# Packed attention and a softplus FFN on one core: batch 0's FFN in two halves around batch 1's

## The chip, the core and the metric

One core of one Trainium2 chip runs the kernel. The metric is device time in microseconds (us), the median of several runs; in the profile, times are counted from the first instruction of the span. Engines: PE (TensorE), DVE (VectorE), ACT (ScalarE), POOL (GpSimd) and SP (SyncE, which here issues nearly all DMAs).

## The reference

```python
def _attn_ref(q, k, v, p):                      # q, k, v: 8 batches, 8 heads, 576 rows, 64 columns
    def sm_attn(qq, kk, vv):                    # softmax attention, scale 1/8
...
    p_packed = sm_attn(p, k, v)                 # p: 32 rows a head
    return sm_attn(q, p_packed, p_packed)

def _moe_ref(x, w_in, w_out):                   # x: 4608 x 512, w_in: 512 x 2048, w_out: 2048 x 512
    h = x @ w_in
    g = np.maximum(h, 0.0) + np.log1p(np.exp(-np.abs(h)))
    return (g @ w_out).astype(np.float32)
```

For each batch, 32 pack rows attend to k and v; then q attends to the 32 packed rows. The heads side by side are x, which goes through a feed-forward net (FFN) with softplus. q, k, v and p come as 32-bit floats, w_in and w_out as 64-bit floats.

## The kernel before, in words

**FFN units.** A batch has 576 rows, and the hidden size 2048 is cut into 16 tiles of 128 (`NF`). A unit (b, f) is one tile of one batch. `gemm1` (L609) makes 12 matmuls 128x288 into two PSUM halves `ph`: softmax weights `at_h`, `at_l` against `mh`, `ml`, the packed rows already multiplied by w_in (`make_m`, L572 to L588). Products are kept exact enough by splitting each factor into a high and a low part, three products each. `softplus` takes abs, exp and ln on ACT (L631, L633, L634), the sum on DVE (L636), copies the last 64 rows to `rest` on POOL (L640) and splits the other 512 into `gh` and `gl` on DVE (L623, L624). Two units later (`LAG`), `gemm2_tile` (L647) adds `gh`, `gl` times `wo_h`, `wo_l` to four accumulators `acc`, three matmuls 128x512 each. There are two `ph` banks, so unit f+1's first half waits for DVE's L636 of unit f. After a batch's last tile, `store` (L662) copies each `acc` to SBUF (L664) and SP writes it out. Each pair of batches has one more accumulator for the `rest` rows.

**Attention ahead.** While a batch's FFN runs, the next batch's attention is done in small steps (`attention_next`, 29 steps), drawn `PACE` = 0.56 steps per accumulator tile. Batch 0's (`attention_first`) comes before all FFN work. `weights` (L545) splits the second softmax's result `aT` into `at_h` (ACT, L554) and `at_l` (DVE, L555), which `gemm1` of that batch needs.

**Conversion.** w_in and w_out are read as 64-bit floats and turned into 32-bit ones in 32 items of 128x512 (`convert`): 16 column blocks of w_in (`i0` to `i15`) and 16 row blocks of w_out (`o0` to `o15`), in the order i0, i1, o0, o1, i2, i3, and so on, counted from 0. An item is a DMA into a buffer `x`, two ACT steps (`m` L204, `r` L208), two DVE steps (`t` L210, L215), one POOL sum (L223), and for w_out a cast on ACT (`wo_h`, L242) and a difference on DVE (`wo_l`, L248). From item 8 on, two buffers of tag `x` hold the items in flight; stores use the same two. Unit (b, f) needs items i`f` and o`f`. Batch 0's FFN draws the conversion's steps at `CONV` = 1.6 per accumulator tile, so all 32 items lie in attention 0 and in batch 0's units.

**What sets the order.** PE and SP keep the program's order. DVE, ACT and POOL get theirs from a scheduler that simulates a timeline when the program is built; from then on it is fixed, and each engine takes its instructions strictly in that order.

## Time and profile before

| | us |
|---|---|
| median of 3 runs (lowest, highest) | 802.3 (802.19, 803.24) |
| profiled execution | 800.31 |
| its span | 798.5 |
| PE busy in the span | 734.1 |
| DVE busy | 542.9 |
| ACT busy | 430.8 |

The time of an execution is the span and 1.8 us around it. A busy PE is not a PE at its peak: the granted clock tells how fast its matmuls run. Unit starts are read from PE's chain: twelve L609 matmuls begin a unit. Batch 0's unit 0 begins at 51.76 us, unit 4 at 95.51, unit 8 at 122.81; batch 1's unit 0 at 173.85, batch 2's at 257.96, batch 3's at 351.87, batch 4's at 434.56.

### The profile page before, as it was taken

Reading aid. Unit: us, or ns where it says so; the run is one execution under the profiler, and the core shown is the slowest. Engines: PE = TensorE matmul, PEld = TensorE weight load, DVE = VectorE, ACT = ScalarE, POOL = GpSimd, SP = SyncE. Lnnn points to the kernel's source line nnn. Section 1 sums busy time; section 2 is a strip of 40 time slices with the busy share of each in tenths; the row PEclk is TensorE's granted clock in tenths of the full one; section 3 lists DMA queues with packets and bytes.
Section 4 is the critical chain, followed back from the end, with each engine's and each line's share of the span. In section 5 each row is a group of like instructions: output and inputs, shape, how many; then the busy total and the mean of one; then the engine's idle time right before and its main releaser. Section 6 shows DMA issues by size and latency. Waiting matters only on the chain.

```text
span 798.5 us, 14178 instructions
## 1 busy us (share of the span) xinstructions
PE 734.1 (92%) x5312; PEld 576.1 (72%) x5312; DVE 542.9 (68%) x1228; ACT 430.8 (54%) x1073; POOL 93.5 (12%) x166
## 2 busy tenths in 40 slices
PE   6423798999999999999999999999999999999997
PEld 3302666676878877887778877887788778778886
DVE  2697787786587666867586666866686656775554
ACT  5646768455546264565555264566456265555540
POOL 1334424100000000010001000010000000000010
PEclk9655799999999999999999999999999999999999
DMA  9979746107310362007200452008200500010002
GB/s 222 237 154 222 188 97 177 37 1 142 61 31 1 83 103 67 1 1 152 58 23 2 106 80 68 1 27 146 61 1 1 126 1 2 1 53 1 1 1 66
DMA packets 168244, 55.96 MB, mean 70 GB/s; under 512 B 134896, under 2 KB 161520, under 8 KB 168176
## 3 DMA queue, kind: packets, MB, share of 16 engines
q1 hardware_dynamic: 167904, 55.00, 31.3%
q8 instruction: 41, 0.67, 0.3%
q14 instruction: 27, 0.22, 0.1%
q10 hardware_dynamic: 272, 0.07, 0.0%
HBM read 45.61 MB, written 9.44 MB: 69 GB/s over the span
## 4 chain that ended last, share of the span: by engine, by line
PE 71%; DVE 10%; DMA 9%; ACT 6%; issue 2%; SPq 1%; POOL 0%; DVEq 0%; ACTq 0%; POOLq 0%
PE acc L647 36%; PE ph L609 23%; PE acc_m L647 6%; DMA x_i<-in_moe_w_in 4%; PE psm L572 3%; DMA x_o<-in_moe_w_out 2%; PE ps L284 2%; DMA v<-in_v 2%; DVE e L636 1%; ACT e L631 1%; ACT e L633 1%; PE psp L327 1%; PE psa L317 1%; DVE t L210 1%; DVE at_l L555 1%
## 5 line engine op out<-in xcount | busy, mean ns | idle before, releaser
L631 ACT ACTIVATE e<-ph 128x288 f32<-128x288 f32 x256 | 102.4, 403 | 201.4 <-PE ph L609 181.5
L647 PE MATMUL acc<-wo_h,gh 128*128 128x512 f32 x512 | 207.8, 406 | 0.2 <-DVE o L664 0.2
L647 PE MATMUL acc<-wo_l,gh 128*128 128x512 f32 x512 | 201.6, 394 | 0.0
L647 PE MATMUL acc<-wo_h,gl 128*128 128x512 f32 x512 | 200.9, 392 | 0.0
L636 DVE SCALAR_TENSOR_TENSOR e<-ph,e 128x288 f32<-128x288 f32 x256 | 113.3, 450 | 121.2 <-ACT e L634 119.9
L609 PE MATMUL ph<-at_h,mh 128*128 128x288 f32 x512 | 160.7, 314 | 34.0 <-DVE e L636 18.2
L609 PE MATMUL ph<-at_l,mh 128*128 128x288 f32 x512 | 154.4, 302 | 3.6 <-DVE at_l L555 3.6
L609 PE MATMUL ph<-at_h,ml 128*128 128x288 f32 x512 | 154.2, 301 | 0.0
L609 PEld LDWEIGHTS ph<-at_h,mh 128*128 128x128 f32 x512 | 98.7, 193 | 72.3 <-DVE e L636 27.3
L640 POOL COPY rest<-e 128x64 f32<-128x64 f32 x128 | 48.1, 376 | 600.4 <-DVE e L636 534.8
L647 PEld LDWEIGHTS acc<-wo_h,gh 128*128 128x128 f32 x512 | 96.6, 189 | 28.6 <-issue 9.8
L647 PEld LDWEIGHTS acc<-wo_h,gl 128*128 128x128 f32 x512 | 96.5, 188 | 21.1
L633 ACT ACTIVATE e<-e 128x288 f32<-128x288 f32 (+1 forms) x240 | 108.7, 454 | 3.4
L634 ACT ACTIVATE e<-e 128x288 f32<-128x288 f32 (+1 forms) x240 | 108.9, 455 | 2.9
L647 PEld LDWEIGHTS acc<-wo_l,gh 128*128 128x128 f32 x512 | 96.8, 189 | 13.3
L609 PEld LDWEIGHTS ph<-at_l,mh 128*128 128x128 f32 x512 | 98.9, 193 | 7.0 <-DVE at_l L555 4.4
L609 PEld LDWEIGHTS ph<-at_h,ml 128*128 128x128 f32 x512 | 99.0, 193 | 0.0
L624 DVE TENSOR_TENSOR gl<-e,gh 128x512 fp32r<-128x512 f32 x128 | 89.9, 703 | 5.8
L587 ACT CAST mh<-psm 128x512 fp32r<-128x512 f32 (+1 forms) x72 | 35.5, 540 | 51.1 <-PE psm L572 51.0
L588 DVE TENSOR_TENSOR ml<-psm,mh 128x512 fp32r<-128x512 f32 (+1 forms) x72 | 42.6, 625 | 29.7 <-ACT mh L587 29.3
L623 DVE CAST gh<-e 128x512 fp32r<-128x512 f32 x128 | 55.3, 432 | 5.7 <-PE acc L647 0.5
L572 PE MATMUL psm<-w_in_sb,pt 64*32 64x512 f32 (+1 forms) x576 | 38.7, 573 | 2.5 <-DVE a L351 1.7
(72 smaller groups left out, 704.6 us busy)
## 6 DMA issues: line engine op xcount, KB each, us to landing
v<-in_v SPq DMA_DIRECT2D x16, 576.0 KB, 4.9
x_i<-in_moe_w_in SPq DMA_DIRECT2D x32, 256.0 KB, 5.0
x_o<-in_moe_w_out SPq DMA_DIRECT2D x16, 512.0 KB, 4.4
q<-in_q SPq DMA_DIRECT2D x56, 144.0 KB, 3.2
k<-in_k SPq DMA_DIRECT2D x52, 144.0 KB, 3.1
out<-o SPq DMA_DIRECT2D x21, 256.0 KB, 2.1
out<-o SPq DMA_DIRECT2D x10, 192.0 KB, 2.3
w_in_sb<-in_k SPq DMA_DIRECT2D x2, 576.0 KB, 5.9
```

Source lines behind the costliest of these rows:

```text
L572: nc.tensor.matmul(ps[hh * J:(hh + 1) * J, :n], res["pt"][g][o:o + D, hh * J:(hh + 1) * J], w_in_sb[o:o + D, hh, c * n:(c + 1) * n], start ...
L587: nc.scalar.copy(mh[:, cols], ps[:, :n])
L588: nc.vector.tensor_tensor(ml[:, cols], ps[:, :n], mh[:, cols].bitcast(F32), op=ALU.subtract)
L609: nc.tensor.matmul(ph[:, :C], x[:, ms], y[:, g, cs], start=(i == 0), stop=(i == 3 * G - 1),)
L623: nc.vector.tensor_copy(hi, x)
L624: nc.vector.tensor_tensor(lo, x, hi.bitcast(F32), op=ALU.subtract)
L631: nc.scalar.activation(es[c], hv[c], AF.Abs)
L633: nc.scalar.activation(x, x, AF.Exp, scale=-1.0)
L634: nc.scalar.activation(x, x, AF.Ln, bias=1.0)
L636: nc.vector.scalar_tensor_tensor(es[c], hv[c], 0.0, es[c], op0=ALU.max, op1=ALU.add)
L640: nc.gpsimd.tensor_copy(rest[:, rest_at(b, f), r:r + REST], e[:, NT * P:])
L647: nc.tensor.matmul(acc, x[:, cs], y[:, f, :], start=(first and i == 0), stop=(last and i == 2),)
```

## The change

- **Order of FFN units** (`runs`): batch 0's tiles 0 to 7, batch 1's 0 to 15, batch 0's 8 to 15, then batches 2 to 7 as before. After tile 7, batch 0's four accumulators are stored to the output; near the end `fetched` reads them back and the last store adds them (`part`).
- **Attention:** batch 1's runs in batch 0's first eight units (`PACE_FIRST` = 0.95), batch 2's from batch 1's tile 8 on (0.56). k of batch 1 is loaded within attention 0. In attention 0, the transposes of q come together and the second softmax is taken for two chunks next to each other.
- **Conversion:** 1.1 steps per accumulator tile until done, with its instructions at a priority lower by 150 for the scheduler.
- **Buffers:** the turned k and q and the weights `at_h`, `at_l` of a batch share two buffers `T0` or `T1`, by batch; items 2, 3, 6 and 7 use `T1` before batch 1 needs it. Turned k of batch 2 goes through the two `x` buffers. Batch 1 makes its `m` for two tiles at a time, like batch 0, no longer for four.
- **Scheduling block:** the simulated timeline covers the program up to batch 2's first unit. There a branch leads into a second block, which the ordinary scheduler orders.

```diff
-    ctx.enter_context(tc.block(schedule_with_timeline_sim=True))
...
-        t = cv.tile([PW, H, D], F32, tag="m", name=f"p_{bg}", bufs=1)
+        t = work.tile([PW, H, D], F32, tag="a1T", name=f"p_{bg}", bufs=1)
...
-        pool, bufs = (cv, 2) if tag == "x" else (work, 1)
+        pool, bufs = (cv, 2) if tag == "x" else (work, 2)
...
-        slots = ["x", "x", "at_h", "at_l"]
+        slots = ["x", "x", "T1", "T1"]
...
+    def place(b):
+
+        return f"T{b if b < 2 else (b + 1) % 2}"
...
-        return work.tile([P, HG, C], F32, tag="T", name=f"T_{nm}_{b}_{g}", bufs=2)
+        return work.tile([P, HG, C], F32, tag=place(b), name=f"T_{nm}_{b}_{g}", bufs=2)
...
-        src, dst = loaded[nm, b, g], turned(nm, b, g)
+        src = loaded[nm, b, g]
+        dst = None if (nm, b) == ("k", 2) else turned(nm, b, g)
+        heads = []
+            two = (
+                cv.tile([P, 2, C], F32, tag="x", name=f"T_{nm}_{b}_{g}_{o}", bufs=2)
+                if dst is None else dst[:, o:o + 2, :]
+            )
...
-        qt = turned("q", b, 0)
-        qT.append(transposed("q", b, 0, 0, qt))
...
-        for hh in range(2, HG):
-            qT.append(transposed("q", b, 0, hh, qt))
-            yield
-        a2 = scores2(b, 0, 0, qT)
-        a2n = scores2(b, 0, 1, qT)
-        yield
...
+        a2 = {}
+        for g in range(G):
+            qt = turned("q", b, g)
+            qT = []
+            for hh in range(HG):
+                qT.append(transposed("q", b, g, hh, qt))
+                yield
+                if (g, hh) == (0, 0):
+                    res[b]["pt"].append(packed_transposed(b, 1, pp[1]))
+                if g and hh < 2:
+                    (softmax2_exp, softmax2_div)[hh](b, 0, 0, a2[0, 0])
+            load("k", b + 1, g)
+            for c in range(2):
+                a2[g, c] = scores2(b, g, c, qT)
+            yield
+        softmax2_exp(b, 1, 0, a2[1, 0])
+        yield
+        softmax2_div(b, 1, 0, a2[1, 0])
+        softmax2_exp(b, 0, 1, a2[0, 1])
+        yield
+        softmax2_div(b, 0, 1, a2[0, 1])
+        softmax2_exp(b, 1, 1, a2[1, 1])
+        yield
+        softmax2_div(b, 1, 1, a2[1, 1])
...
+        def load_next(nm, g):
+            if b > FIRST:
+                load(nm, b + 1, g)
-        load("k", b + 1, 0)
+        load_next("k", 0)
...
-        for nm, g in (("k", 0), ("k", 1), ("q", 0), ("v", 0), ("v", 1), ("q", 1)):
+        if b > FIRST:
+            for nm in ("k", "v"):
+                for g in range(G):
+                    load(nm, b, g)
+                    for _ in range(4):
+                        yield
+            return
+        for nm, g in (("q", 0), ("v", 0), ("v", 1), ("q", 1)):
             load(nm, b, g)
-            for _ in range(4):
+            for _ in range(3):
...
-        at_h = work.tile([P, G, S], F32R, tag="at_h", name=f"at_h_{b}", bufs=1)
-        at_l = work.tile([P, G, S], F32R, tag="at_l", name=f"at_l_{b}", bufs=1)
+        at_h, at_l = (
+            work.tile([P, G, S], F32R, tag=place(b), name=f"{nm}_{b}", bufs=2)
+            for nm in ("at_h", "at_l")
+        )
...
-        return MC if b else MC // 2
+        return MC if b > 1 else MC // 2
...
-        pool, th, tl = (cv, "t", "r") if b and c % 2 == 0 else (work, "mh", "ml")
+        pool, th, tl = (cv, "t", "r") if b > 1 and c % 2 == 0 else (work, "mh", "ml")
...
-    def store(acc, pieces, nm):
-        o = cv.tile([P, DM], F32, tag="x", name=f"o_{nm}", bufs=2)
-        nc.vector.tensor_copy(o, acc)
...
+    def fetched():
+
+        two = [
+            cv.tile([P, 2, DM], F32, tag="x", name=f"part_{i}", bufs=2) for i in range(NT // 2)
+        ]
+        parts = [two[t // 2][:, t % 2, :] for t in range(NT)]
+        for t, o in enumerate(parts):
+            move(o, [(0, 0, t * P, P)], False)
+        return parts
+
+    def store(acc, pieces, nm, part=None):
+        if part is None:
+            o = cv.tile([P, DM], F32, tag="x", name=f"o_{nm}", bufs=2)
+            nc.vector.tensor_copy(o, acc)
+        else:
+            o = part
+            nc.vector.tensor_tensor(o, acc, o, op=ALU.add)
+        move(o, pieces, True)
...
+    HALF = NF // 2
     PACE = 0.56
-    AFTER = 10
-    CONV = 1.6
+    PACE_FIRST = 0.95
+    BEHIND = 150
+    CONV = 1.1
+
+    front = ExitStack()
+    front.enter_context(tc.block(schedule_with_timeline_sim=True))
+
+    def convert_on():
+        with tc.high_priority(offset=-BEHIND):
+            next(conv, None)
...
-            next(conv)
+            convert_on()
...
-    early = loads(FIRST)
-    units = [(b, f) for b in range(B) for f in range(NF)]
-    ahead, chain, due = iter(()), iter(()), 0.0
+    early = iter(())
+    runs = [(0, 0, HALF), (1, 0, NF), (0, HALF, NF)] + [(b, 0, NF) for b in range(2, B)]
+    units = [(b, f) for b, f0, f1 in runs for f in range(f0, f1)]
+    starts = {(b, f0): f1 for b, f0, f1 in runs}
+    ends = {(b, f1 - 1): f0 for b, f0, f1 in runs}
+    ahead, chain, due, pace = iter(()), iter(()), 0.0, 0.0
...
+            if b == 2 and f == 0:
+                front.close()
+            begins = {(0, 0): 1, (1, HALF): 2}.get((b, f), b + 1 if b > 1 and f == 0 else B)
+            if (b, f) == (0, NF - 2):
+                parts = fetched()
+            if (b, f) in ((0, 0), (1, 2)):
+                early = loads(b + 1)
...
+                due, pace = 0.0, PACE if begins > 1 else PACE_FIRST
             chain = softplus(b, f, gemm1(b, f, res[b]), gs)
+            if (b, f) in ends and u + 1 < len(units) and (b, f) != (1, NF - 1):
                 for _ in ahead:
                     pass
-                if b + 1 < B:
-                    weights(b + 1)
+                weights(units[u + 1][0])
...
+            if (b2, f2) in starts:
+                acc = [
+                    ps_acc.tile([P, DM], F32, tag="acc", name=f"acc_{b2}_{f2}_{t}")
+                    for t in range(NT)
+                ]
+        done = u >= LAG and (b2, f2) in ends
+        last = done and f2 == NF - 1 and (b2 == 0 or b2 > 1 and b2 % 2)
...
+                if done:
+                    part = parts[t] if (b2, f2) == (0, NF - 1) else None
+                    store(acc[t], [(0, b2, t * P, P)], f"{b2}_{f2}_{t}", part)
...
-                if b < FIRST:
-                    next(early, None)
-                due += PACE if b >= FIRST or NT * f + t >= AFTER else 0
+                next(early, None)
+                due += pace
...
-                if b == 0:
-                    cdue += CONV
-                    while cdue >= 1:
-                        next(conv, None)
-                        cdue -= 1
+                cdue += CONV
+                while cdue >= 1:
+                    convert_on()
+                    cdue -= 1
```

**How instructions move: ACT around batch 0's unit 4.** `e_0_4` is the softplus of batch 0's tile 4; `m_n` and `r_n` are the two ACT steps of conversion item n, `x_o10` is item 22's buffer. Before:

```order
L204 ACTIVATE m_22_1102<-x_o10_1001 128x512
L208 ACTIVATE r_23_1133<-x_o11_1049 128x512
L631 ACTIVATE e_0_4_822<-ph_0_4_0_808 128x288
L204 ACTIVATE m_23_1131<-x_o11_1049 128x512
L631 ACTIVATE e_0_4_822<-ph_0_4_1_815 128x288
L633 ACTIVATE e_0_4_822<-e_0_4_822 128x576
L242 CAST wo_h_91<-t_22_1106 128x512
L208 ACTIVATE r_24_1178<-x_i12_1108 128x512
L634 ACTIVATE e_0_4_822<-e_0_4_822 128x576
L204 ACTIVATE m_24_1176<-x_i12_1108 128x512
L587 CAST mh_0_3_0_880<-psm_0_3_0_870 128x256
L242 CAST wo_h_91<-t_23_1135 128x512
```

The same place with the change (`a1T_1` and `a1_1` belong to batch 1's attention):

```order
L645 ACTIVATE e_0_3_800<-e_0_3_800 128x576
L328 COPY a1T_1_1_876<-psa_1_1_0_877 96x384
L642 ACTIVATE e_0_4_896<-ph_0_4_0_882 128x288
L642 ACTIVATE e_0_4_896<-ph_0_4_1_889 128x288
L644 ACTIVATE e_0_4_896<-e_0_4_896 128x576
L328 COPY a1T_1_1_876<-psa_1_1_1_906 96x384
L645 ACTIVATE e_0_4_896<-e_0_4_896 128x576
L598 CAST mh_0_3_0_989<-psm_0_3_0_979 128x256
L598 CAST mh_0_3_0_989<-psm_0_3_1_980 128x256
L642 ACTIVATE e_0_5_1009<-ph_0_5_0_995 128x288
L642 ACTIVATE e_0_5_1009<-ph_0_5_1_1002 128x288
L644 ACTIVATE e_0_5_1009<-e_0_5_1009 128x576
```

In both programs items 0 to 21 have their `m` and `r` on ACT ahead of `e_0_4`. Before, items 22 to 25 follow from the middle of `e_0_3` to `e_0_5`; now none stands from there to batch 1's `e_1_2`.

**SP around item 22 (`x_o10`).** Before:

```order
L162 DMA x_i10_933<-in_moe_w_in 64x4x128 x2
L162 DMA x_i11_955<-in_moe_w_in 64x4x128 x2
L162 DMA x_o10_1001<-in_moe_w_out 128x512
L162 DMA x_o11_1049<-in_moe_w_out 128x512
L162 DMA x_i12_1108<-in_moe_w_in 64x4x128 x2
L162 DMA x_i13_1137<-in_moe_w_in 64x4x128 x2
L149 DMA k_2_0_1170<-in_k 32x36x32 x4
L162 DMA x_o12_1182<-in_moe_w_out 128x512
L149 DMA k_2_1_1273<-in_k 32x36x32 x4
L162 DMA x_o13_1290<-in_moe_w_out 128x512
```

With the change (`o_0_7_t` is batch 0's partial sum, accumulator t after tile 7):

```order
L161 DMA x_i10_1232<-in_moe_w_in 64x4x128 x2
L161 DMA x_i11_1280<-in_moe_w_in 64x4x128 x2
L678 DMA out_0<-o_0_7_0_1343 96x512
L678 DMA out_0<-o_0_7_0_1343 32x512
L161 DMA x_o10_1353<-in_moe_w_out 128x512
L678 DMA out_0<-o_0_7_1_1358 64x512 x2
L678 DMA out_0<-o_0_7_2_1367 32x512
L678 DMA out_0<-o_0_7_2_1367 96x512
L678 DMA out_0<-o_0_7_3_1380 96x512
L678 DMA out_0<-o_0_7_3_1380 32x512
L161 DMA x_o11_1391<-in_moe_w_out 128x512
```

The load of item 22 now stands behind the first store of the partial sums, and item 23's behind all of them. On ACT, item 22's `m` and `r` stand within `e_1_2`, batch 1's tile 2, item 23's within `e_1_3`; each has softplus steps behind it in the queue. The buffers alternate, so `o_0_7_2` takes item 22's.

**DVE where batch 1's FFN begins.** Before, `at_l_1` is finished ahead of the softplus sum of batch 0's last tile:

```order
L371 TENSOR_TENSOR a2_1_1_1_1644<-a2_1_1_1_1644,z2_1_1_1_1748 128x288
L588 TENSOR_TENSOR ml_1_0_1_1721<-psm_1_0_1_1707,mh_1_0_1_1720 128x512
L375 STREAM_TRANSPOSE aT_1_1_0_1693<-a2_1_1_0_1637 128x288
L375 STREAM_TRANSPOSE aT_1_1_1_1753<-a2_1_1_1_1644 128x288
L555 TENSOR_TENSOR at_l_1_1756<-aT_1_0_0_1555,at_h_1_1755 128x288
L555 TENSOR_TENSOR at_l_1_1756<-aT_1_0_1_1622,at_h_1_1755 128x288
L555 TENSOR_TENSOR at_l_1_1756<-aT_1_1_0_1693,at_h_1_1755 128x288
L555 TENSOR_TENSOR at_l_1_1756<-aT_1_1_1_1753,at_h_1_1755 128x288
L116 COPY pT_94<-ppt_1_0_1782 64x256
L636 SCALAR_TENSOR_TENSOR e_0_15_1738<-ph_0_15_0_1724,e_0_15_1738 128x288
```

With the change, the end of batch 1's second softmax stands among the last steps of batch 0's tile 7, directly ahead of batch 1's first softplus sum:

```order
L634 CAST gh_0_7_1239<-e_0_7_1183 128x512
L381 TENSOR_TENSOR a2_1_1_0_1124<-a2_1_1_0_1124,z2_1_1_0_1190 128x288
L379 TENSOR_SCALAR z2_1_1_1_1201<-z2_1_1_1_1201 128x9
L635 TENSOR_TENSOR gl_0_7_1240<-e_0_7_1183,gh_0_7_1239 128x512
L385 STREAM_TRANSPOSE aT_1_1_0_1195<-a2_1_1_0_1124 128x288
L380 RECIPROCAL z2_1_1_1_1201<-z2_1_1_1_1201 128x9
L381 TENSOR_TENSOR a2_1_1_1_1131<-a2_1_1_1_1131,z2_1_1_1_1201 128x288
L566 TENSOR_TENSOR at_l_1_1209<-aT_1_1_0_1195,at_h_1_1208 128x288
L385 STREAM_TRANSPOSE aT_1_1_1_1206<-a2_1_1_1_1131 128x288
L566 TENSOR_TENSOR at_l_1_1209<-aT_1_1_1_1206,at_h_1_1208 128x288
L647 SCALAR_TENSOR_TENSOR e_1_0_1262<-ph_1_0_0_1248,e_1_0_1262 128x288
```

From the first transpose of that last softmax group (`a2_1_1_0`) to the last `at_l_1`, 29 DVE instructions stand in this queue; on PE, one more unit (0, 7), three matmuls L647 and one `make_m` stand between the scores that start them and batch 1's first `gemm1`.

More of the change, by code (lines that the diff above doesn't have):

```diff
@@ L499, in attention_next @@
         yield
-        load("k", b + 1, 1)
+        load_next("k", 1)
         a1T = work.tile([NP, SI, P], F32, tag="a1T", name=f"a1T_{b}_1", bufs=1)
@@ L508, in attention_next @@
         yield
-        load("v", b + 1, 0)
+        load_next("v", 0)
         a2 = scores2(b, 0, 0, qT[0])
@@ L514, in attention_next @@
         yield
-        load("v", b + 1, 1)
+        load_next("v", 1)
         softmax2_exp(b, 0, 0, a2)
@@ L660, in rows, with move @@
         return n, o.rearrange("(t c) e -> c t e", c=2)[c, t:t + n, :]
-    def store(acc, pieces, nm):
-        o = cv.tile([P, DM], F32, tag="x", name=f"o_{nm}", bufs=2)
-        nc.vector.tensor_copy(o, acc)
+    def move(o, pieces, to_dram):
         for row, b, col, n in pieces:
             while n:
-                m, dst = rows(b, col, n)
-                nc.sync.dma_start(dst, o[row:row + m, :])
+                m, at = rows(b, col, n)
+                here = o[row:row + m, :]
+                nc.sync.dma_start(*((at, here) if to_dram else (here, at)))
                 row, col, n = row + m, col + m, n - m
+    def fetched():
[14 more added lines that the diff above has]
+        move(o, pieces, True)
     def rests(b):
@@ L754, in pack_attention_then_softplus_ffn @@
             gh, gl = gs.pop((b2, f2))
-            if f2 == 0:
-                acc = [ps_acc.tile([P, DM], F32, tag="acc", name=f"acc_{b2}_{t}") for t in range(NT)]
-        last = u >= LAG and f2 == NF - 1 and b2 % 2 == 1
+            if (b2, f2) in starts:
[5 more added lines that the diff above has]
+        last = done and f2 == NF - 1 and (b2 == 0 or b2 > 1 and b2 % 2)
         if last:
-            both = rests(b2)
+            both = rests(b2 + 1 - b2 % 2)
             next(both)
@@ L763, in pack_attention_then_softplus_ffn @@
                 gemm2_tile(
-                    acc[t], gh, gl, f2, slice(t * P, (t + 1) * P), f2 == 0, f2 == NF - 1
+                    acc[t], gh, gl, f2, slice(t * P, (t + 1) * P), (b2, f2) in starts, done
                 )
-                if f2 == NF - 1:
-                    store(acc[t], [(0, b2, t * P, P)], f"{b2}_{t}")
+                if done:
+                    part = parts[t] if (b2, f2) == (0, NF - 1) else None
+                    store(acc[t], [(0, b2, t * P, P)], f"{b2}_{f2}_{t}", part)
             if u < len(units):
-                if b < FIRST:
-                    next(early, None)
-                due += PACE if b >= FIRST or NT * f + t >= AFTER else 0
+                next(early, None)
+                due += pace
                 while due >= 1:
```

45 lines of the change are left out of this document (10 added, 35 removed).

## The prediction

> **What bounds the kernel now.** I read the page first: its span, the busy times and the slices of 20 us.
>
> ```profile
> span 798.5 us, 14178 instructions
> PE 734.1 (92%) x5312; PEld 576.1 (72%) x5312; DVE 542.9 (68%) x1228; ACT 430.8 (54%) x1073; POOL 93.5 (12%) x166
> PE   6423798999999999999999999999999999999997
> PEclk9655799999999999999999999999999999999999
> ```
>
> PE is the bound from the seventh slice on. Its 64 us of idle time lie almost wholly in the first six slices, where its clock is low too. So only the front can give time back. The view of busy times in stretches, cut at the starts of units, says how much. Its columns are the stretch, its length, then busy time of PE, weight loads, DVE, ACT and POOL, the granted clock and the share of the DMA engines.
>
> ```profile
> 20.00:51.76 31.76, 12.17 (x128) 7.41 (x129) 25.23 (x52) 19.31 (x41) 11.06 (x8) 0.59 0.86 215
> 51.76:95.51 43.75, 20.49 (x104) 15.36 (x105) 34.58 (x67) 27.37 (x53) 17.95 (x15) 0.62 0.86 196
> 95.51:122.81 27.30, 24.60 (x167) 18.57 (x167) 21.52 (x45) 18.37 (x41) 8.13 (x9) 0.91 0.53 114
> 122.81:173.85 51.04, 47.25 (x400) 35.13 (x401) 41.17 (x102) 31.56 (x66) 10.27 (x13) 0.97 0.28 72
> 173.85:257.96 84.11, 82.27 (x622) 64.82 (x622) 58.51 (x135) 47.26 (x125) 5.68 (x16) 1.00 0.28 56
> 173.85:182.64 8.79, 8.79 (x49) 7.79 (x49) 5.56 (x12) 4.89 (x13) 1.12 (x2) 1.00 0.04 10
> 351.87:434.56 82.69, 82.19 (x624) 64.83 (x622) 58.89 (x136) 47.62 (x126) 6.43 (x16) 1.00 0.28 57
> ```
>
> Rows two to four are batch 0's sixteen units: 122.09 us, where batch 3 (last row) takes 82.69 with PE busy all the time. The excess is 39.4 us. The sixth row holds two bare units, without attention: 4.39 us each. Units 0 to 3 take 43.75 where four bare ones take 17.6, so most of the excess, 26 us, lies there. What the first units wait for, the waits from 51.8 to 174 us and the chain from 60 to 140 us show.
>
> ```profile
> PE ph L609 <- DVE e L636: 16.1, 7, 8.1
> ACT r L208 <- DMA x_i<-in_moe_w_in: 6.5, 5, 2.9
> ```
>
> ```profile
> 70.23 6.63 DMA x_i<-in_moe_w_in
> ...
> 78.74 3.91 DMA x_o<-in_moe_w_out
> ...
> 85.93 4.75 DMA x_i<-in_moe_w_in
> ...
> 95.00 0.47 DVE e L636
> ...
> 95.51 3.25 PE ph L609 x12
> ...
> 108.19 2.28 PE acc L647 x9
> ```
>
> PE waits for the softplus sum on DVE, DVE for ACT, and ACT stands at a conversion item whose DMA has not landed, with softplus steps behind it. The conversion's queue position, not its amount, stalls PE here.
>
> **The change part by part.** I sum from unit to unit, against the profiled execution: it took 800.31 us, 1.8 more than its span and 2.0 less than the median of 802.3. Batch 2 starts at 257.96 us; from there on the work is the same, so the change in time is the change of that start, plus what the second block costs.
>
> *A, up to unit 4 of batch 0 (95.51).* On ACT, items 0 to 21 still stand ahead of unit 4's softplus, so the stall of units 0 to 3 isn't removed, only its cause can shrink. DVE is busy for 34.58 of 43.75 us; 9.2 are idle. The change moves the first part of batch 1's attention in here. Its DVE groups (51.8 to 174 us):
>
> ```profile
> L260 DVE STREAM_TRANSPOSE T_q<-q 128x576 f32<-128x576 f32 x4 | 2.9, 752 | 0.0
> L297 DVE TENSOR_REDUCE m<-a 128x1 f32<-128x576 f32 x2 | 1.5, 726 | 0.0
> ```
>
> With small ones that is 2.9 + 1.5 + 0.5 = 4.9 us more. Against it, batch 1's v and its last q leave this stretch: by SP's order they now go out ahead of item 14, mostly between 20 and 51.76 us, where the DMA engines have 14% free, and the three chained landings of 15.3 us get shorter. Bounds: 4.3 earlier (all idle time filled) to 4.9 later (none). I take 1.5 earlier, for the DMA waits are the larger sum: 94.0.
>
> *B, units 4 to 7.* Before: 27.30 us, with conversion items and a little attention. Now no conversion step stands there, but batch 1's attention must end there. Four bare units are 17.6; attention and its matmuls cost 82.69 − 16 × 4.39 = 12.4 us a batch, half of it here: 6.2. At the end PE waits for `at_l_1`: 29 DVE instructions, at 58.89 / 136 = 0.43 us each 12.6 us, while PE has one bare unit, three matmuls L647 (2.28 / 9 × 3 = 0.8) and one `make_m` of 0.95, 6.1 in all; the latter from
>
> ```profile
> L572 PE MATMUL psm<-w_in_sb,pt 64*32 64x256 f32 (+1 forms) x96 | 5.7, 458 | 2.5 <-DVE a L351 1.7 <-DVE pp L335 0.8
> ```
>
> (six of them). The wait is 0 to 6.5 us; not all 29 stand before the first matmul, so I take 4. B is 27.8: nothing is won here, though the attention is now done.
>
> *C, batch 1's tiles 0 to 7.* Eight bare units and four `make_m` are 35.1 + 3.8 = 38.9 us. Ten conversion items lie in them and just behind. The waits come from the landing times of DMA issues (last number, us; the store in the third row) and from durations by group (ACT and DVE from 51.8 to 174 us, L664 from batch 3):
>
> ```profile
> x_i<-in_moe_w_in SPq DMA_DIRECT2D x32, 256.0 KB, 5.0
> x_o<-in_moe_w_out SPq DMA_DIRECT2D x16, 512.0 KB, 4.4
> out<-o SPq DMA_DIRECT2D x21, 256.0 KB, 2.1
> ```
>
> ```profile
> L204 ACT ACTIVATE m<-x_o 128x512 f32<-128x512 f32 x11 | 7.3, 665 | 2.8 <-DMA x_o<-in_moe_w_out 1.7 <-DVE t L215 0.9
> L208 ACT ACTIVATE r<-x_o 128x512 int32<-128x512 uint32 x10 | 6.7, 674 | 4.6 <-DMA x_o<-in_moe_w_out 4.5
> ```
>
> ```profile
> L215 DVE SCALAR_TENSOR_TENSOR t<-m,t 128x512 int32<-128x512 int32 x22 | 15.0, 682 | 0.3
> L210 DVE TENSOR_SCALAR t<-m 128x512 int32<-128x512 int32 x21 | 11.0, 524 | 10.1 <-ACT m L204 10.0
> ...
> L664 DVE COPY o<-acc 128x512 f32<-128x512 f32 x4 | 2.8, 689 | 1.4 <-PE acc L647 1.4
> ```
>
> Item 22's load follows the first store of batch 0's sums on SP: copy 0.7, landing 4.4, `m` and `r` 1.3, copy of the third sum 0.7: 7.1 us, while PE has five tiles of 0.76 and one `gemm1`, 4.39 − 4 × 0.76 = 1.3: 5.1 in all. That is 2 us of waiting for the accumulator. Item 23 follows a store in the same buffer (2.1 + 4.4 + 1.3), and waits about as long; the other eight take a round of some 6 us in two buffers, 3 an item, and a unit lasts 4.9, so mostly they are hidden. Bounds 0 and 10 × (6.0 − 4.9) plus those two, 15; I take 4.5: C is 43.4.
>
> *D, batch 1's tiles 8 to 15 and batch 0's.* Sixteen units with one attention, as in batch 3: 82.7. Item 31's load must wait until batch 2's first scores free its buffer, and softplus stands behind it on ACT: 4.4 + 1.3 against the rest of a unit, 0 to 5, I take 2. D is 84.7.
>
> *E, the clock.* A gap costs more than itself:
>
> ```profile
> 144.79 1.35 PE L572 MATMUL psm<-w_in_sb,pt 64*32 64x256 f32 x16 [1.71 <-DVE a L351]
> ```
>
> ```profile
> 140.00:150.00 10.00, 8.29 (x102) 5.65 (x102) 8.04 (x19) 3.50 (x8) 2.00 (x2) 0.83 0.33 74
> ```
>
> After 1.71 us of waiting the clock fell to 0.83 over ten, 1.7 us lost. Units 4 to 7 lost 9% of 27.30 before, 2.5. I take 2.5 in all, bounds 0 and 7. [...]
>
> *F, the second block.* One taken branch per engine, and the order of DVE and ACT from there. No row shows a branch in midstream. Bounds 0 and the landing of a load, 5.0; I take 0.5, as one per engine is all. Batch 3's PE has 82.19 of 82.69 busy, so its order has slack and I take nothing for it. [...]
>
> The second pass over `acc` is hidden: four more stores, and four reads issued a unit ahead into buffers that are free, at a DMA share of 0.28; an addition takes a copy's place on DVE. Uncovered, four more copies would cost 2.8.
>
> Sum: 94.0 + 27.8 + 43.4 + 84.7 + 2.5 + 0.5 = 252.9 against 257.96: 5.1 us less. On the profiled execution that is 795.2, on the median 797.2.
>
> **The rivals.** *The waits are hidden.* DVE's 12.6 us run shorter back to back and loads land sooner while the DMA is idle: the 4, 4.5 and 2 of B, C and D and 1 of E go, 11.5 more: 785.7. For it: DVE has 0.43 us an instruction with its start-up in it. Against: fixed queues, short slack.
>
> *The gain is eaten up*: A comes out later, as DVE has 4.9 us more, and waits are a little larger: within 1.6 us of before. For it: A's bounds.
>
> *The conversion stalls batch 1 (slower).* If rounds don't overlap, as each buffer is given to a store or a turned k in between, an item costs landing 4.7, `m`, `r` 1.3 and 1.2 for the two steps of `t` on DVE, 7.2 us against a unit of 4.9: 2.3 for seven items, 16 in C instead of 4.5, and 2.5 more of E. That is 14 − 5.1 = 8.9 us slower, 811.2. It decides once a round is longer than a unit and nothing overlaps it. For it: the chained landings before. Against: item 24 on has two buffers.
>
> *The second block is worse ordered.* One gap of 1.7 us per batch in the last six is 10 us: 807. Against: PE's 82.19 of 82.69.
>
> **How the numbers follow.** Forecast, 2 to 11 us faster: 0.40 (791 to 800). Waits hidden: 0.12. Eaten up: 0.13. Conversion stalls: 0.27. Second block: 0.08. About 0.2%, 1.6 us, is what a measurement of this kernel can tell from no change. Faster is 0.40 + 0.12 = 0.52, same 0.13, slower 0.35. Both signs are likely; the range, 785 to 811, reaches the two far rivals and leaves out their outer halves.
>
> **What would show it.** In the profile after: unit 4 of batch 0 at about 94 us (A); a PE gap of about 4 us ahead of batch 1's first L620 matmuls, released by `at_l` (B), there near 122; gaps of about 2 us in batch 1's tiles 2 and 3, released by a copy of `acc` and by `e`, with ACT waiting for `x_o` (C); batch 2's start at 253; PE without idle time from there. I am wrong if unit 4 comes after 98, if batch 1's first eight units take over 50 us, or if PE has gaps in batches 3 to 7.

## The result, and the profile after

The changed kernel takes 814.13 us (median of 4 runs, 811.36 to 814.98) where the kernel before takes 802.25: a ratio of 1.0148, 95% interval 1.0112 to 1.0185. It is slower, by 12 us where 5 less were forecast. The profiled execution took 811.36 us, its span 809.6.

The page of the changed kernel:

```profile
span 809.6 us, 14353 instructions
PE 741.9 (92%) x5376; PEld 580.9 (72%) x5376; DVE 548.4 (68%) x1240; ACT 436.1 (54%) x1081; POOL 92.0 (11%) x166
PE   6523898879899999999999999999999999999997
DMA  9997200782253053203340343005230500010002
```

PE is at 7 in the ninth slice, 162 to 182 us, and at 8 in the seventh, eighth and eleventh, where before it was at 9 from the eighth on. The DMA engines almost stand still in the sixth and seventh slices (101 to 142 us) and are at 7 and 8 again in the eighth and ninth: that is the conversion's last part, now in batch 1.

The changed kernel's busy times in stretches, cut at the starts of units: units 0 to 3 of batch 0 (A), 4 to 7 (B), batch 1's tiles 0 to 7 (C), the sixteen units up to batch 2 (D), and the rest. Columns as in the prediction.

```profile
51.78:102.62 50.84, 28.04 (x193) 19.96 (x194) 40.74 (x89) 31.67 (x63) 20.31 (x17) 0.63 0.60 146
102.62:126.04 23.42, 23.14 (x217) 16.86 (x214) 17.16 (x49) 13.05 (x28) 0.81 (x3) 1.00 0.01 2
126.04:181.77 55.73, 44.00 (x266) 33.46 (x265) 36.84 (x74) 32.28 (x78) 12.40 (x15) 0.94 0.62 149
181.77:271.93 90.16, 87.08 (x687) 66.71 (x687) 65.29 (x151) 53.05 (x126) 10.29 (x19) 0.98 0.31 70
271.93:809.60 537.67, 532.72 (x3775) 427.48 (x3774) 359.34 (x823) 277.24 (x726) 35.69 (x97) 1.00 0.22 46
```

Before, the stretches with the same counts of units took 43.75, 27.30, 51.04, 84.11 and 540.54 us. So A is 7.1 longer, B 3.9 shorter, C 4.7 and D 6.0 longer, and the rest 2.9 shorter: 11.1 us in all, the difference of the spans.

**A.** SP's instructions from 50 to 70 us show what stands ahead of a conversion item (start, time that the issues took, line):

```profile
50.23 0.38 SPq L136 DMA_DIRECT2D v<-in_v  x1
...
54.00 0.55 SPq L136 DMA_DIRECT2D v<-in_v  x1
56.84 1.25 SPq L161 DMA_DIRECT2D x_i<-in_moe_w_in  x2
58.19 6.18 SPq L148 DMA_DIRECT2D q<-in_q  x4
64.47 1.64 SPq L161 DMA_DIRECT2D x_o<-in_moe_w_out  x2
```

The chain of waits there, and ACT's instructions behind it:

```profile
57.49 6.64 DMA x_i<-in_moe_w_in
...
64.47 4.34 DMA x_o<-in_moe_w_out
...
70.81 4.05 DMA x_i<-in_moe_w_in
...
82.95 3.97 DMA x_i<-in_moe_w_in
```

```profile
68.92 0.66 ACT L203 ACTIVATE m<-x_o 128x512 f32<-128x512 f32 x1 [0.22 <-DMA x_o<-in_moe_w_out]
69.48 0.65 ACT L207 ACTIVATE r<-x_o 128x512 int32<-128x512 uint32 x1
70.04 0.67 ACT L644 ACTIVATE e<-e 128x576 f32<-128x576 f32 x1
```

q's four DMAs keep SP's queue for 6.18 us, the item's load behind them goes out at 64.47, and unit 0's exp (L644) stands behind its `m` and `r`. Unit 0 itself, 21.14 us long, would be almost as long without these loads, as e4 shows below; what is delayed is the items, whose landings units 1 to 3 still wait for (from 70.81 and from 82.95).

**C.** The longest waits of ACT, and then of PE, in that stretch:

```profile
ACT m L203 <- DMA x_o<-in_moe_w_out: 5.3, 3, 3.0
...
ACT m L203 <- DMA x_i<-in_moe_w_in: 1.7, 2, 1.0
```

```profile
PE ph L620 <- DVE e L647: 6.0, 4, 3.5
PE acc L658 <- DVE o L694: 3.1, 2, 2.0
PE ph L620 <- ACT at_h L565: 2.4, 1, 2.4
```

The first PE row is softplus behind items on ACT, the second the copies of `acc` into `x` buffers, the third the wait at batch 1's first matmul. Behind three places with gaps lies a stretch at half clock (the last three columns are the clock, the DMA share and GB/s; the gap ahead of the last row is the one of 3.5 us; in the middle row a matmul 128x512 followed the one before after 0.43 us, at a clock of 1.00 from 152.39 us on after 0.23):

```profile
126.04:130.42 4.38, 1.93 (x11) 1.32 (x10) 3.84 (x13) 0.93 (x3) 0.24 (x1) 1.00 0.00 0
130.42:133.83 3.41, 3.41 (x10) 2.72 (x10) 1.43 (x4) 2.43 (x6) 0.13 (x1) 0.50 0.00 0
...
147.49:150.90 3.41, 3.41 (x23) 1.61 (x22) 2.28 (x5) 0.87 (x2) 0.82 (x2) 0.50 0.56 165
...
181.62:185.03 3.41, 3.26 (x13) 3.18 (x14) 3.28 (x7) 3.25 (x9) 1.66 (x2) 0.50 0.01 2
```

**D.** The matmuls of `make_m` in this stretch, after, and then in the same stretch before:

```profile
L583 PE MATMUL psm<-w_in_sb,pt 64*32 64x256 f32 (+1 forms) x128 | 6.9, 415 | 1.1 <-ACT a1T L328 0.9 <-DVE pt L352 0.3
```

```profile
L572 PE MATMUL psm<-w_in_sb,pt 64*32 64x512 f32 x64 | 4.4, 601 | 0.0
```

Batch 1's `m` is now made two tiles at a time, with twice the matmuls at 415 ns instead of 601: 2.5 us more. Of the other 3.5 us of D, 1.3 are more idle time of PE, and some 1.8 lost clock (0.98 over 90.16 us).

### The profile page after: what moved, and what is told of

Its sections match the earlier page's. It is cut to its first block, busy times and chain, and to the rows that moved or that the text cites. A ratio compares the mean times of both kernels' runs of the same rounds, so it can differ in the third digit from the quotient of the medians.

```text
span 809.6 us, 14353 instructions
## 1 busy us (share of the span) xinstructions
PE 741.9 (92%) x5376; PEld 580.9 (72%) x5376; DVE 548.4 (68%) x1240; ACT 436.1 (54%) x1081; POOL 92.0 (11%) x166
## 4 chain that ended last, share of the span: by engine, by line
PE 78%; DMA 9%; DVE 7%; ACT 3%; issue 1%; SPq 1%; DVEq 0%; ACTq 0%
PE acc L658 40%; PE ph L620 24%; DMA x_i<-in_moe_w_in 6%; PE acc_m L658 5%; PE psm L583 4%; PE ps L294 2%; DMA x_o<-in_moe_w_out 2%; PE psp L337 1%; PE psa L327 1%; DMA out<-o 1%; DVE e L647 1%; DVE t L209 1%; ACT m L203 1%; DVE t L214 1%; DVE a L361 1%
## 5 line engine op out<-in xcount | busy, mean ns | idle before, releaser
L647 DVE SCALAR_TENSOR_TENSOR e<-ph,e 128x288 f32<-128x288 f32 x256 | 112.7, 451 | 126.4 <-ACT e L645 123.1
L644 ACT ACTIVATE e<-e 128x288 f32<-128x288 f32 (+1 forms) x240 | 109.1, 456 | 3.6
L634 DVE CAST gh<-e 128x512 fp32r<-128x512 f32 x128 | 57.3, 448 | 5.6
L583 PE MATMUL psm<-w_in_sb,pt 64*32 64x512 f32 (+1 forms) x640 | 41.7, 537 | 1.4 <-ACT a1T L328 0.9
```

The lines of the kernel that those rows point to most:

```text
L583: nc.tensor.matmul(ps[hh * J:(hh + 1) * J, :n], res["pt"][g][o:o + D, hh * J:(hh + 1) * J], w_in_sb[o:o + D, hh, c * n:(c + 1) * n], start ...
L634: nc.vector.tensor_copy(hi, x)
L644: nc.scalar.activation(x, x, AF.Exp, scale=-1.0)
L647: nc.vector.scalar_tensor_tensor(es[c], hv[c], 0.0, es[c], op0=ALU.max, op1=ALU.add)
```

## The experiments

The first theory: A is long through batch 1's loads ahead of items on SP, C through the ten items' DMA rounds in two buffers, and the second block gives 2.9 us. Its rivals: DVE's work makes A long; the items' work, not their loads, makes C long. The table has each run's ratio to the kernel before with its 95% interval, and the lengths of A to D and of the rest from its profile. The first unit's start moved between 48.7 and 54.7 us from profile to profile, so lengths are compared, not starts. Each length is from one profile: A, for one, is between 48.77 and 52.84 us in the changed kernel and the six whose edit hardly bears on units 0 to 3 (e2, e5, e6, e9, e13, e14), so a difference of 2 us in one stretch says little.

| run | ratio (interval) | A | B | C | D | rest |
|---|---|---|---|---|---|---|
| before | 1 | 43.75 | 27.30 | 51.04 | 84.11 | 540.5 |
| changed | 1.0148 (1.0112, 1.0185) | 50.84 | 23.42 | 55.73 | 90.16 | 537.7 |
| e1 | 0.9965 (0.9944, 0.9986) | 43.57 | 27.64 | 51.18 | 84.11 | 537.3 |
| e2 | 1.0208 (1.0173, 1.0244) | 52.84 | 23.40 | 56.35 | 91.79 | 543.2 |
| e3 | 1.0052 (1.0025, 1.0078) | 45.92 | 34.11 | 49.69 | 87.11 | 537.9 |
| e4 | 1.0095 (1.0060, 1.0130) | 43.99 | 23.40 | 62.37 | 88.64 | 537.7 |
| e5 | 1.0128 (1.0094, 1.0162) | 51.61 | 23.40 | 54.30 | 92.23 | 537.6 |
| e6 | 1.0124 (1.0078, 1.0170) | 50.93 | 23.38 | 58.14 | 91.25 | 538.0 |
| e7 | 1.0005 (0.9985, 1.0024) | 45.82 | 31.61 | 48.44 | 87.12 | 537.6 |
| e8 | 0.9967 (0.9945, 0.9989) | 45.54 | 25.32 | 53.64 | 84.77 | 537.3 |
| e9 | 1.0117 (1.0081, 1.0153) | 51.40 | 35.56 | 46.59 | 87.13 | 537.7 |
| e10 | 1.0049 (1.0031, 1.0067) | 44.49 | 31.39 | 50.90 | 87.44 | 538.0 |
| e11 | 0.9960 (0.9940, 0.9980) | 46.02 | 28.21 | 46.41 | 85.87 | 537.5 |
| e12 | 0.9954 (0.9934, 0.9975) | 45.63 | 26.71 | 51.59 | 83.77 | 537.3 |
| e13 | 1.0005 (0.9984, 1.0027) | 48.77 | 23.39 | 51.79 | 87.15 | 537.7 |
| e14 | 0.9942 (0.9922, 0.9963) | 51.62 | 23.39 | 45.72 | 87.15 | 537.7 |
| e15 | 0.9830 (0.9813, 0.9846) | 44.84 | 22.68 | 46.49 | 84.27 | 537.3 |
| e16 | 0.9949 (0.9931, 0.9968) | 46.24 | 28.02 | 54.76 | 83.94 | 537.3 |

### The second block: e1 and e2

e1 is the kernel before with the block split:

```diff
-    ctx.enter_context(tc.block(schedule_with_timeline_sim=True))
+    front = ExitStack()
+    front.enter_context(tc.block(schedule_with_timeline_sim=True))
...
+            if b == 2 and f == 0:
+                front.close()
```

> The kernel before, with one part of the change alone: the scheduled block ends ahead of batch 2's first unit, and a second one holds the rest. Nothing else differs. Theory: in the changed kernel the stretch from batch 2's start to the end is 537.67 us against 540.54 before, and this comes from the order that DVE and ACT have in a second block; so this kernel has batch 2's start near 258 us as before, the stretch behind it near 537.7, and is about 2.9 us faster than before (ratio near 0.9964). Rival: those 2.9 us come from the order of the FFN tiles (buffers that come free in another rhythm), and the block alone gives nothing: ratio 1.000, stretch 540.5.

e2 is the changed kernel with `front.close()` taken out and one block over all.

> The changed kernel with one scheduled block over the whole program, as before; all else as in the changed kernel. Theory: the second block is worth the 2.9 us behind batch 2's start, and the front (271.93 us in the changed kernel) stays: about 817 us, 1.0035 of the changed kernel's time. Rival: the shorter block also changes the order in the front, so the front differs by more than 3 us, in either direction.

The last stretch of e1, and of e2, and then batches 2 and 3 of the changed kernel:

```profile
259.84:797.10 537.26, 532.48 (x3774) 427.71 (x3774) 361.10 (x823) 276.17 (x727) 36.74 (x97) 1.00 0.22 46
```

```profile
275.61:818.80 543.19, 534.79 (x3774) 427.11 (x3774) 356.90 (x819) 277.49 (x726) 34.55 (x97) 1.00 0.22 45
```

```profile
271.93:365.68 93.75, 93.74 (x679) 74.06 (x678) 66.58 (x157) 47.36 (x124) 5.78 (x17) 1.00 0.28 55
365.68:447.44 81.76, 81.76 (x624) 65.07 (x623) 58.58 (x135) 48.09 (x126) 5.23 (x16) 1.00 0.30 57
```

e1 came out as expected: A to D within 0.4 us of before, the rest 3.3 us shorter, the kernel faster than before (800.24 us against 802.43). In e2 (820.28 us) the rest is 5.5 us longer than in the changed kernel, but A to D together are 4.2 longer too, so its rival may hold beside its theory. In batches 2 and 3 of the second block PE has no idle time left: batch 3 takes 81.76 us, where it took 82.69 before with PE busy for 82.19. So the second block is the one part of the change that is shown to win, in either order of the FFN. The second pass over `acc` is hidden, as forecast: the changed kernel's rest is 537.67, and e1's, which has no second pass, 537.26.

### Units 0 to 3: e4, e3, e8

e4, with v and the second q of batch 1 not loaded:

```diff
+        if b == 1 and (nm, g) in (("v", 0), ("v", 1), ("q", 1)):
+            loaded[nm, b, g] = loaded[(nm, 0, g) if nm == "v" else (nm, 1, 0)]
+            return
```

> The changed kernel without three loads of batch 1 (both v and the second q; batch 0's v and batch 1's first q are used in their place, so this leaves out part of the computation's input and does the same work on other data). Theory: unit 4 of batch 0 comes at 102.62 us instead of 94 because these loads go ahead of conversion item 14 on SP and hold it for 6 us or more; without them it comes at 95 to 98, and the kernel is 4 to 8 us faster than the changed one, 806 to 810. Rival: DVE's additional work of batch 1's attention in units 0 to 3 makes them long, and unit 4 stays at 101 or later.

Stretches A and C of e4:

```profile
51.67:95.66 43.99, 25.59 (x194) 17.24 (x194) 40.82 (x87) 31.75 (x63) 17.77 (x16) 0.68 0.45 131
...
119.06:181.43 62.37, 47.80 (x265) 35.74 (x264) 39.35 (x80) 33.70 (x80) 13.51 (x17) 0.89 0.57 133
```

Without the loads A is 43.99, 6.9 us shorter with the same DVE work (40.82 us against 40.74): the loads are the cause of these 6.9 us, and the rival falls. They are lost in units 1 to 3, here in the changed kernel and then in e4:

```profile
72.92:102.62 29.70, 21.91 (x165) 16.65 (x166) 23.27 (x49) 19.82 (x41) 11.76 (x11) 0.72 0.34 96
```

```profile
72.44:95.66 23.22, 19.46 (x166) 13.93 (x166) 21.64 (x46) 18.85 (x39) 8.95 (x10) 0.84 0.37 107
```

Unit 0 takes 21.14 us in the one and 20.77 in the other, so it isn't what the loads make long; in kernels with the old order of tiles it is 17.22 (before), 20.21 (e8) and 22.42 (e12, with the new order of attention 0). The kernel without the loads took 810.89 us, where 806 to 810 were expected: it won only some 3 us, since C grew by 6.6. ACT's waits for items there grew too:

```profile
ACT m L206 <- DMA x_o<-in_moe_w_out: 7.9, 4, 2.7
...
ACT m L206 <- DMA x_i<-in_moe_w_in: 3.4, 2, 2.0
```

Its scheduled order differs from the changed kernel's, and why C lost as much as A had won stays open.

e3 draws all conversion steps in batch 0's eight units, which also puts items 12 to 15 ahead of loads of batch 1 that they followed:

```diff
-    CONV = 1.1
+    CONV = 2.0
```

> The changed kernel with 2.0 instead of 1.1 conversion steps per tile of the FFN: on SP's queue items 22 to 31 then stand ahead of the first stores of batch 0's partial sums, and none is left for batch 1. Theory: batch 1's first eight units took 55.7 us, 12.3 more than forecast, because ten items go round two buffers behind stores; without them they take 40 to 44 us. Units 4 to 7 of batch 0 grow from 23.4 us to 27 to 31, as the items stand there. Sum: 5 to 11 us less than the changed kernel, 803 to 809 us. Rival: the length of those eight units has another cause (gaps at the border of the batches and their clock windows), so they stay over 50 us and the kernel gets no faster.

Its stretches B and C:

```profile
96.86:130.97 34.11, 27.36 (x216) 19.42 (x214) 30.90 (x74) 23.90 (x48) 12.93 (x12) 0.90 0.46 132
130.97:180.66 49.69, 42.71 (x266) 33.78 (x264) 32.72 (x65) 24.86 (x63) 7.05 (x12) 0.93 0.48 90
```

A is 45.92 with all the loads, at a DMA share of 0.74 against 0.60: what stands behind the loads on SP makes A long, more than their traffic. Two items still have their ACT steps in C. The time, 807.35, was as expected, but with other terms: units 4 to 7 took 34.11, as DVE is busy for 30.90 of them with the items and batch 1's attention, and C 49.69, with waits of 3.4 us for `at_h` and 1.6 for `at_l` and a mean clock of 0.93.

e8 is e1 with six empty steps ahead of the loads:

```diff
     def loads(b):
+        for _ in range(6):
+            yield
```

> The kernel before with the second block alone (800.24 us) and, besides, batch 1's six loads six tiles later on SP: three conversion items more stand ahead of the first of them. Theory: where a load of q, k or v stands ahead of a conversion item on SP, that item comes later by several us, and softplus behind it on ACT, and PE behind that; so units 0 to 3, 43.6 us in the kernel it is made from, take 39 to 42 us, and the kernel is 1 to 4 us faster, 796 to 799. Rival: the items' own rounds set the pace there, and the loads take idle DMA time: no difference, 800.

Units 0 to 3 of e8, and of e1:

```profile
51.76:97.30 45.54, 21.71 (x105) 16.25 (x105) 36.91 (x69) 27.43 (x53) 17.99 (x15) 0.93 0.96 198
```

```profile
53.34:96.91 43.57, 20.55 (x104) 15.45 (x104) 34.59 (x67) 27.62 (x53) 18.11 (x15) 0.62 0.88 196
```

No gain (800.03), as its rival had it: in the old order the sequence of the loads is not what bounds these units. Whether the traffic is, at a DMA share of 0.88 to 0.96, e11 asks below.

### Batch 1's first eight units: e5, e6, e9, e13, e14

e5 takes the partial sums out of the `x` buffers, e6 sets `BEHIND = 0`:

```diff
-            o = cv.tile([P, DM], F32, tag="x", name=f"o_{nm}", bufs=2)
+            pool, tag = (work, "a1") if nm.startswith("0_7") else (cv, "x")
+            o = pool.tile([P, DM], F32, tag=tag, name=f"o_{nm}", bufs=2)
```

> The changed kernel with the four partial sums of batch 0's first half copied into the two buffers of tag a1, which nobody uses then, instead of the two x buffers of the conversion. Theory 1: the ten conversion items of batch 1 are slow because their loads stand behind those copies and stores; then the waits for the accumulator (1.08 and 2.02 us in the changed kernel) and the half-clock window behind them (1.7 us) go, and the following items come earlier: the first eight units of batch 1 take 46 to 50 us instead of 55.7, and the kernel 807 or less. Theory 2: the loads' own round (issue, landing, m and r, next issue) of 4 to 5 us an item sets the pace, with softplus behind each item on ACT; then only 1 to 3 us are won there, and later units of the eight lose part of it again: 811 to 814.

> The changed kernel with conversion steps at normal priority instead of 150 behind. Theory: the low priority moves DVE's and ACT's conversion steps only a few places, since the order of their loads on SP is fixed by the program, so the front changes by less than 3 us in either direction. Rival: the low priority is what delays the items and so the rounds in batch 1's first units; then that stretch (55.7 us) is shorter by 5 us or more at normal priority.

e5: C 54.30, 1.4 us shorter, D 2.1 longer, 812.03: sharing the buffers with stores is not the cause, and its second theory held. e6: 812.96; the low priority isn't the cause either. Then the loads of items 22 to 31 were left out, their steps reading `wo_h` (e9):

```diff
+            if 22 <= n < len(order):
+                xs[n] = wo_h[:, 0:2, :].rearrange("x a n -> x (a n)")
+            elif n < len(order):
```

> The changed kernel without the loads of conversion items 22 to 31: their m and r read a part of wo_h in SBUF instead, so ACT, DVE and GpSimd do the same work on other data and only the DMA rounds are gone (those weights are wrong, which leaves that part of the computation out). Theory: in batch 1's first eight units ACT stands at items whose load has not landed, with softplus behind, and that is most of the 12 us that they take beyond the forecast; without the loads they take 42 to 46 us instead of 55.7, batch 2 starts at 257 to 262, and the time is 799 to 804. Rival: the items' work on ACT and DVE is what delays softplus, loads or not; then they take 50 us or more, and the time is 808 or more.

Stretches B and C of e9:

```profile
103.35:138.91 35.56, 27.79 (x214) 19.77 (x214) 33.42 (x74) 24.66 (x48) 13.62 (x13) 0.86 0.01 2
138.91:185.50 46.59, 42.70 (x264) 33.51 (x264) 27.18 (x59) 21.89 (x58) 3.17 (x9) 0.93 0.51 90
```

812.19, which the intervals can't tell from the changed kernel: against the theory, and C isn't the 50 us of the rival either. The items' work had moved into B, where DVE is busy 33.42 of 35.56 us; C is down to 46.59. So two kernels followed: e13 reads `at_h` of batch 1 in place of the loads, which holds the work in batch 1, and e14 has no items 22 to 31 at all; the tiles that need them use the weights of earlier tiles.

```diff
-            x = xs.pop(n)
+            x = xs.pop(n) if n < 22 else res[1]["at"][0].rearrange("x g s -> x (g s)")[:, :2 * CN]
```

> The changed kernel without the loads of items 22 to 31, as the run before that read wo_h; but their m and r now read at_h of batch 1, so that no item can be done ahead of batch 1's first matmuls (in that other run the ten items moved into units 4 to 7: these took 35.56 us instead of 23.42, and batch 1's first eight 46.59 instead of 55.73, with nothing won in the sum). Again the weights are wrong and the work on ACT, DVE and GpSimd the same. Theory 1 (rounds): units 4 to 7 take 23 to 25 us, batch 1's first eight 44 to 48, and batch 2 starts at 260 to 264: 801 to 805. Theory 2 (work: wherever ten items lie, some 10 us of PE's waiting lie too): batch 1's first eight take 52 us or more, 809 or more.

```diff
+    del order[22:]
...
+        c0 = min(c * n, 12 * P - n)
...
-                    w_in_sb[o:o + D, hh, c * n:(c + 1) * n],
+                    w_in_sb[o:o + D, hh, c0:c0 + n],
...
-                acc, x[:, cs], y[:, f, :],
+                acc, x[:, cs], y[:, f if f < 10 else f - 6, :],
```

> The changed kernel without conversion items 22 to 31 at all: the tiles that would need their weights use those of earlier tiles (part of the conversion is left out, the result differs, the matmuls are the same). Theory 1 (rounds): 1 to 3 us less than with the items' work but no loads (the run beside this one), batch 1's first eight units 42 to 45 us. Theory 2 (work): the ten items' own work costs 8 to 12 us, so batch 1's first eight take 42 to 45 us here, and 52 or more there.

Stretches C and D of e13, and of e14:

```profile
124.69:176.48 51.79, 43.21 (x265) 33.64 (x264) 44.32 (x86) 35.37 (x84) 17.85 (x19) 0.93 0.44 81
176.48:263.63 87.15, 85.30 (x689) 65.30 (x687) 57.62 (x141) 49.25 (x118) 5.49 (x15) 1.00 0.26 59
```

```profile
129.67:175.39 45.72, 41.30 (x265) 32.97 (x264) 27.09 (x60) 22.00 (x58) 3.16 (x9) 0.96 0.48 91
175.39:262.54 87.15, 85.29 (x688) 65.33 (x687) 57.52 (x141) 49.24 (x118) 5.49 (x15) 1.00 0.26 59
```

PE's waits in C, of e13 and then of e14:

```profile
PE ph L620 <- DVE e L647: 6.0, 4, 3.6
PE ph L620 <- ACT at_h L565: 2.3, 1, 2.3
```

```profile
PE ph L621 <- ACT at_h L565: 2.4, 1, 2.4
PE ph L621 <- DVE e L648: 1.3, 1, 1.3
```

Neither theory holds alone. C and D together are 145.89 us in the changed kernel, 138.94 in e13 and 132.87 in e14: the items' loads cost 7.0 us (3 of it in D, where the last items lie), their work on ACT and DVE 6.1. PE's 6.0 us of waiting for `e` are in e13 as in the changed kernel, so these can be put down to the items' work; what goes with the loads in C are the 3.1 us for `acc`. The split is rough: by the ratios of the whole times the two parts are 11.5 and 5.1 us. That both count holds either way.

### What the order of the FFN's tiles is worth: e10, e11, e15

e10 leaves out the loads of items 14 to 31 as e9 did from 22, e11 does that to e1, and e15 takes items 22 to 31 out of e1 as e14 did.

> The changed kernel without the loads of items 14 to 31 (their m and r read a part of wo_h instead; those weights are wrong). To be set against the next run, which is the same in the old order. Theory: with the rounds gone from units 0 to 3 as well, unit 4 comes at 92 to 97 and batch 2 at 247 to 256. The new order by itself is then worth nothing or less: it has 2.5 us more of make_m matmuls (128 of 256 columns at 415 ns against 64 of 512 at 601) and the wait ahead of batch 1's first matmul with its half-clock window (4 us), against which stands only that DVE has room in batch 1; so its batch 2 comes 2 to 7 us later than in the next run. Rival: the order is good and only the loads spoil it; then batch 2 comes 3 us or more earlier than in the next run.

> The kernel before with the second block (800.24 us), without the loads of items 14 to 31 as in the run ahead of this one. Theory: units 0 to 3 took 43.6 us at a DMA share of 0.88, so the loads bound them; without, unit 4 comes at 84 to 90 and batch 2 at 245 to 252: 786 to 793. Rival: ACT's and DVE's work bounds these units: unit 4 stays at 93 or later and the time at 797 or more.

> The kernel before with the second block (800.24 us), without items 22 to 31 in the same way. It shows what the order of the FFN's tiles is worth by itself when ten items don't matter. Theory: with the items out the new order still pays 2.5 us for make_m in 256 columns, some 4 us for the wait and half-clock window at batch 1's first matmul, and 6 us for the place of batch 1's loads on SP, and gains what DVE has free in batch 1; here batch 2 starts at 248 to 254, in the new order without the ten items at 256 to 262. Rival: the new order is the better one once the items are out, and its batch 2 starts earlier than here.

Stretches A, C and D of e15:

```profile
54.53:99.37 44.84, 21.42 (x105) 15.99 (x105) 35.18 (x67) 26.44 (x51) 17.70 (x15) 0.65 0.80 168
...
122.05:168.54 46.49, 44.68 (x403) 33.94 (x400) 33.38 (x88) 24.66 (x52) 2.98 (x8) 1.00 0.12 30
168.54:252.81 84.27, 82.21 (x623) 64.78 (x623) 56.39 (x131) 47.59 (x125) 5.21 (x16) 1.00 0.28 56
```

A to D of e14 sum to 207.9 us and of e15 to 198.3. With the ten items gone, the new order is still 9.6 us behind: 6.8 in A, 2.9 in D (`make_m`, 2.5), and B and C together level. The 6.8 fit the 6.9 of the loads in e4, but 5.9 of them lie in unit 0 (23.08 us against 17.22), where e4 saw next to nothing of the loads, so the cause of A's part isn't shown here. Without loads from item 14 on, it is 7.7 behind (e10 214.2, e11 206.5). Both sums were above what was expected: batch 2 began at 265.90 us in e10 (247 to 256 forecast) and at 259.13 in e11 (245 to 252). So the order itself wins nothing here. And the items are not cheaper in it: in the old order they cost 8.2 us (e1 206.5, e15 198.3), in the new 12.3 (changed 220.2, e14 207.9); by the ratios it is 10.8 and 16.5. e11 went against its theory: A stayed at 46.02 without those loads, and A to D are 206.5 us with them (e1) and without (e11). By these sums the loads from item 14 on cost nothing in the old order; it is the items' work on ACT and DVE that costs there.

### Parts put together: e7, e12, e16

e7 is e5 with `cdue += 2.0 if u < 4 else 1.1`, so that five items are left for batch 1.

> The changed kernel with 2.0 conversion steps a tile in units 0 to 3 (1.1 from then on, as before) and the four partial sums in the buffers of tag a1. Only items 27 to 31 are then left for batch 1. Theory: unit 4 comes at about 97 as with 2.0 throughout (its loads stand in the same places there), units 4 to 7 take 25 to 29 us (five items instead of eleven), batch 1's first eight 46 to 50, the rest as in the changed kernel: batch 2 starts at 258 to 263, the time is 800 to 805, between the changed kernel and the kernel before with its second block alone (800.2). Rival: what is won in one stretch is lost in the next, because DVE and ACT have the same sum of work to do by batch 2's start; then it is 806 or more, as with 2.0 throughout.

802.81 us, as expected, and the same as before the change: against the changed kernel 5.0 us are won in A, 7.3 in C and 3.0 in D, and 8.2 lost in B, which took 31.61 us where 25 to 29 were expected, with DVE busy for 28.08 of them. e12 is e1 with the changed kernel's order of attention 0; e16 has the low priority as well.

> The kernel before with the second block, and the changed kernel's order of batch 0's attention (second softmax of both groups side by side) as the second part of the change; the order of the FFN's tiles and the conversion stay as before. Theory: the FFN's first unit comes about 1 us earlier (51 against 52 to 53), but units 1 to 4 are set by conversion items' loads, so the time is that of the second block alone, 799 to 801. Rival: the earlier attention lets everything behind it move up, and the time is 2 us or more less: 798 or below.

> The kernel before with the second block and the new order of batch 0's second softmax (798.94 us), and the conversion steps of low priority too: all of the change but the order of the FFN's tiles and what goes with it. Theory: the low priority is worth less than 2 us either way, as in the changed kernel (812.96 at normal priority against 814.13), so 797 to 801. Rival: softplus gets ahead of items on ACT and DVE, and the front gets 3 us or more shorter: 796 or less.

e12 took 798.94 and e16 800.39 us, ratios 0.9954 and 0.9949: both beat the kernel before, but neither can be told from e1 (0.9965). The old order of tiles with the second block is the better kernel.

## Why the prediction was wrong

- **A (94.0 forecast, 102.62 measured): the step that failed first.** "mostly between 20 and 51.76 us, where the DMA engines have 14% free", was said of batch 1's v and last q, as a help to A. In fact v's second part went out at 54.00 and q at 58.19, in the middle of A, and an item waited for them. With them left out A is 43.99 (e4), so they cost 6.9 of the 8.6 us, in units 1 to 3. In e7 these loads go out within A too, but items 12 to 15 stand ahead of those that they followed, and A is 45.82. The forecast's gain of 1.5 from shorter landings didn't come. 102.62 is past the 98 that was named.
- **"The conversion's queue position, not its amount, stalls PE here"**, the premise under A and C, holds for the changed kernel's A (e3, e4), but not for the kernel before, of which it was said. There three items more ahead of the loads win nothing (e8), nor does leaving out the items' loads from 14 on (A to D 206.5 in e1 and e11), while ten items left out altogether give 8.2 us (e15).
- **B (27.8, measured 23.42)** was better, with hardly a wait. The 4 us put there for `at_l` came as 2.36 at `at_h`, inside C; attention 1 ended in time.
- **C, D and E (43.4 + 84.7 + 2.5 = 130.6, measured 145.89): the largest miss, 15.3 us.** The gaps were of the kinds named, but C's 4.5 us for waits was sized by the items' loads alone, with most of the rounds hidden. The sum had 4.5 + 2 for the items' waits and 2.5 for the clock, 9.0 in all. The items cost 13.0, about 7.0 for the rounds and 6.1 for their work on ACT and DVE in batch 1's order, which the sum had at nothing (e13, e14). Without any of the ten (e14) C and D are still 132.87 us, 11.3 more than the 38.9 + 82.7 without waits: in C 4.4 us of waits, 2.4 of them at `at_h`, and about 1.8 of lost clock; in D 1.9 of PE's idle time and the 2.5 of `make_m`'s smaller matmuls, which D's 82.7, "as in batch 3", left out. 13.0 and 11.3 less the 9.0 are the 15.3. C's 55.73 is past the 50 that was named.
- **E**, inside this sum: C at 0.94 and D at 0.98 are 3.3 + 1.8 = 5.1 us of lost clock, twice the 2.5 (estimates from the mean clock). The changed kernel's waits of 2.36 us, and of 1.08 and 2.02 us close together, and a gap of 3.49 us were each followed by 3.41 us at half clock; that at 171.39 us, of 1.33 us, was not. What decides which gap is followed by one isn't shown here.
- **F (0.5 forecast)** had the wrong sign: the second block wins 2.9 us (3.3 in e1). No run shows the 0.5 taken for the branches, nor that one costs a landing of 5.0; in the changed kernel's trace PE is busy from 265 us to the border at 271.93 without a gap, and for 93.74 of the 93.75 us behind it. The step that failed is "so its order has slack and I take nothing for it": batch 3 became 0.9 us shorter, 0.5 of it the idle time that PE had there; the rest stays open.
- **The rival "the conversion stalls batch 1"** gave 811.2, and the profiled execution took 811.36. It was right on the place and near on C: 38.9 + 16 against 55.73. But it laid all of this to the rounds, which are about half, and its total was hit by luck: A's miss of 8.6 was about balanced by B (4.4) and F (3.4).

That sums up: 8.6 - 4.4 + 15.3 - 3.4 = 16.1 us beyond the forecast of 795.2 for the profiled execution.
